# One of sixteen P slabs and one of sixteen dS slabs per attention head: transposed on TensorE instead of by the DMA crossbar

## The chip, the cores and the metric

The kernel runs on one core of one Trainium2 chip. The metric is device time in microseconds, one number per execution. All runs quoted here are of the same state, called fast, and are medians of several executions. The kernel before was run again beside every set of experiments. Its median moved between 5479 and 5498 us from set to set, so kernels of different sets are compared by their ratio to the kernel before of the same rounds, not by their microseconds. A ratio is the mean time of one kernel's fast runs over the mean of the other's fast runs of the same rounds, so it is not quite the ratio of the two medians quoted.

## The reference

The reference is the forward and backward pass of attention gated by a gated linear unit; only attention matters here. It has 32 heads, 2048 queries, 2048 cached keys, head size 128:

```python
q = (x @ wq).reshape(B, Sq, H, Dh).transpose(0, 2, 1, 3)
scores = jnp.einsum("bhqd,bhkd->bhqk", q, k_cache) * Dh ** -0.5
p = softmax(scores)
o = jnp.einsum("bhqk,bhkd->bhqd", p, v_cache)
# ... and the gradients of x, k_cache, v_cache, wq, wo and the gated unit's weights
```

The backward pass needs, per head, `dP = dO V^T`, `dS = P * (dP - delta)`, `dQ = dS K`, `dK = dS^T Q`, `dV = P^T dO`.

## The kernel before

A head is 32 *slots*: 16 P slots, then 16 dS slots, one for each slab of 128 queries. A P slot computes one slab `Pq` (128 x 2048 bf16) of exponentials. A dS slot overwrites it with dS. The products O and dQ need the slab transposed, and one DMA through the crossbar does that for each of the 32 slabs:

```python
def transpose_slab(hs, qt, name):
    T = wpt.tile([P, NT, P], bf, name=name, tag="PT")      # 7 buffers
    nc.sync.dma_start_transpose(T[:], hs.slabs[qt][:])
    return T
```

The transposed slab is used five slots later (`skew = 5`) by a *tail* of 16 matmuls. Each slot also has its share of dV and dK, which read the slab untransposed. From dS slot 6 of a head on, the next one is prepared (the code is cut at each `...`):

```python
def plan(h):
    b1, b2 = 2 * NT * h, 2 * NT * h + NT         # first P slot, first dS slot
    ...
    put(pl + q(skew + 1), 0, lambda: heads.__setitem__(h, prep_loads(h)))   # loads K, V, wq, wo
    put(pl + q(skew + 3), NT * P, lambda: prep_kt(hd()))
    ...
    for qt in range(NT):
        put(b1 + qt + skew, ..., lambda qt=qt: tail1(hd(), qt, 0))          # O
    ...
        put(b2 + qt + skew, ..., lambda qt=qt: tail2(hd(), qt, 0))          # dQ

def prep_loads(h):
    ...
    hs.Vn = ld1.tile([P, NT, P], bf, name="Vn")                             # one buffer
    nc.gpsimd.dma_start(hs.Vn[:], A_v_cache[0, h].rearrange("(p t) d -> p t d", t=NT))   # 512 KB
```

`Vn` has one buffer, so its load for the next head waits for the last O tail, which runs in dS slot 4.

## Time and profile before

| What | Where it is read | Value |
|---|---|---|
| time | three runs | 5479 us (5477 to 5485) |
| attention stage | first and last slot in the timeline | 608 to 3883 us |
| one head | starts of the slots, heads 1 to 30 | mean 103.0 us, median 102.0 us |
| TensorE busy in the stage | windows | 95% |
| pitch (start to start) of 128-column matmuls | starts in the timeline | 55.8 ns |
| TensorE idle per head, by releaser | idle before instructions, heads 2 to 28 | dST 1.9, PT 0.8, VectorE's dS multiply 1.6, small gaps 1.1 us |

The windows of the kernel before, heads 4 to 27. After the length come the busy microseconds of TensorE, its weight loads, VectorE, ScalarE and GpSimd, then the granted clock (the share of TensorE's full clock that the profile records), the DMA share (the packets' time as a share of 16 engines' time, over 1 where packets overlap) and GB/s:

```profile
1012.00:3487.00 2475.00, 2348.21 (x29909) 1868.24 (x30389) 1409.92 (x3154) 1612.02 (x2727) 771.92 (x1325) 1.00 1.14 199
```

TensorE is 2348 / 2475 = 95% busy. The costliest groups of the kernel before; after the bars stand busy time, mean duration, and TensorE's idle time before them with its releaser:

```profile
L535 PE MATMUL dp<-VT,dOT 128*128 128x512 bf16 x1728 | 541.5, 380 | 53.7 <-DVE Pq L538 53.6
L510 PE MATMUL acc<-Kn,dST 128*128 128x128 bf16 x8192 | 554.0, 220 | 69.3 <-DMA dST<-Pq 65.6
L510 PE MATMUL acc<-Vn,PT 128*128 128x128 bf16 x8192 | 547.8, 219 | 33.0 <-DMA PT<-Pq 25.6
```

The dQ tails waited 66 us and the O tails 26 us for a landing from the crossbar, over all heads. The timeline of SP, the engine that issues the transposes, shows why (start, length, count):

```profile
1147.04 25.15 SPq L460 DMA_TRANSPOSE PT<-Pq  x9
1172.29 53.55 SPq L460 DMA_TRANSPOSE dST<-Pq  x16
1225.92 49.98 SPq L460 DMA_TRANSPOSE PT<-Pq  x16
1276.00 15.35 SPq L460 DMA_TRANSPOSE dST<-Pq  x4
```

There is no gap: 16 transposes take 50 to 54 us, the length of the 16 slots. From the end of the instruction that finishes a slab to the issue of its transpose, a P slab waits 3.8 us and a dS slab 4.8 us in the median. So two resources are nearly full, TensorE and the transposing queue.

### The profile page before, as it was taken

The page shows a single profiled execution, that of the slowest core. Times are in us where ns is not written, and L with a number is a line of the kernel's source. Part 1 is how long each engine was busy: PE and PEld are TensorE (multiplying, and loading weights), DVE is VectorE, ACT ScalarE, POOL GpSimd, SP SyncE. Part 2 cuts the span into 40 slices and gives each one's busy share as a digit, 9 for nine tenths or more (in the row PEclk, how much of TensorE's full clock was granted, in tenths as well). Part 3 has the DMA queues.
Part 4 walks back from the last instruction along what each step waited for, and adds up shares of the span by engine and source line. Part 5 has one row for each costly group of instructions (what it writes and reads, how often), then busy time and mean ns, then how long its engine had stood idle before and what let it go on. Part 6 is the DMA issues. An engine that isn't in the chain of part 4 may idle for free. (4 is left out here: it accounts for less than half of the span.)

```text
span 5498.0 us, 129982 instructions
## 1 busy us (share of the span) xinstructions
PE 5095.5 (93%) x54343; PEld 3654.3 (66%) x55220; DVE 2497.0 (45%) x5692; ACT 2695.0 (49%) x4794; POOL 1420.1 (26%) x2361
## 2 busy tenths in 40 slices
PE   8878899999999999999999999999789999899999
PEld 3334577777777777777777777777557777644454
DVE  4443455655655555655556555555333333210011
ACT  7751466666666666666666666666222222100000
POOL 2212323323333233333233233223112222211000
PEclk9999999999999999999999999999999999999999
DMA  7658799999999999999999999999945455674865
GB/s 282 235 187 194 155 199 189 204 196 201 200 200 198 200 198 193 200 205 199 201 200 199 188 199 198 200 198 189 236 143 195 167 174 180 199 219 120 172 146 111
DMA packets 2721787, 1053.95 MB, mean 192 GB/s; under 512 B 2521937, under 2 KB 2642386, under 8 KB 2719138
## 3 DMA queue, kind: packets, MB, share of 16 engines
q1 hardware_dynamic: 2637890, 764.83, 76.0%
q0 software_dynamic: 83296, 280.64, 16.6%
q8 instruction: 434, 7.11, 0.5%
q14 instruction: 167, 1.37, 0.1%
HBM read 213.91 MB, written 201.00 MB: 75 GB/s over the span
## 5 line engine op out<-in xcount | busy, mean ns | idle before, releaser
L484 ACT ACTIVATE Pq<-sp 128x1024 bf16<-128x1024 f32 x1024 | 1048.1, 1024 | 328.2 <-PE sp L466 205.5
L570 PEld LDWEIGHTS <-Pq 128*128 128x128 bf16 x16384 | 1002.5, 98 | 241.2 <-issue 2.1
L542 ACT ACTIVATE t<-dp,negdelta 128x1024 bf16<-128x1024 f32 x512 | 571.5, 1116 | 278.9 <-POOL negdelta L524 160.7
L538 DVE SCALAR_TENSOR_TENSOR Pq<-dp,delta,Pq 128x1024 bf16<-128x1024 f32 x512 | 655.0, 1279 | 58.1 <-PE acc L510 56.4
L510 PE MATMUL acc<-Kn,dST 128*128 128x128 bf16 x8192 | 554.0, 220 | 69.3 <-DMA dST<-Pq 65.6
L510 PEld LDWEIGHTS <-PT 128*128 128x128 bf16 x8192 | 498.8, 98 | 156.4 <-DMA PT<-Pq 47.8
L543 DVE TENSOR_TENSOR Pq<-t,Pq 128x1024 bf16<-128x1024 bf16 x512 | 419.1, 819 | 398.1 <-ACT t L542 394.9
L535 PE MATMUL dp<-VT,dOT 128*128 128x512 bf16 x1728 | 541.5, 380 | 53.7 <-DVE Pq L538 53.6
L510 PEld LDWEIGHTS <-dST 128*128 128x128 bf16 x8192 | 490.4, 98 | 140.3 <-DMA dST<-Pq 85.7
L510 PE MATMUL acc<-Vn,PT 128*128 128x128 bf16 x8192 | 547.8, 219 | 33.0 <-DMA PT<-Pq 25.6
L570 PE MATMUL acc<-dOn,Pq 128*128 128x128 bf16 x8192 | 546.5, 219 | 10.3 <-DVE o_n L50 0.2
L466 PE MATMUL sp<-KT,QT 128*128 128x512 bf16 x1762 | 547.7, 379 | 1.2 <-ACT Pq L484 1.2
L570 PE MATMUL acc<-Qn,Pq 128*128 128x128 bf16 x8192 | 541.3, 219 | 3.4
L499 POOL TENSOR_SCALAR dOn<-dOn,rinv_all 128x128 bf16<-128x128 bf16 x512 | 313.9, 613 | 612.0 <-DVE rinv_all L472 502.9
L552 ACT ACTIVATE dq_n<-acc,rsc 128x128 bf16<-128x128 f32 x512 | 188.3, 368 | 401.8 <-PE acc L510 401.8
L800 PEld LDWEIGHTS <-xn_all 128*128 128x128 bf16 (+1 forms) x2880 | 281.5, 100 | 40.3 <-issue 11.1
L50 DVE TENSOR_SCALAR o_n<-acc,rinv_all 128x128 bf16<-128x128 f32 x352 | 123.5, 351 | 299.3 <-PE acc L510 299.3
L580 POOL DMA_DIRECT2D out_dram<-kvo x256 | 148.9, 582 | 406.3 <-DVE kvo L579 404.0
L276 PE MATMUL g_ps<-wg_sb,xnT 128*128 128x512 bf16 x694 | 185.8, 392 | 59.8 <-ACT oma L282 50.2
L504 POOL DMA_DIRECT2D dq_d<-dq_n x128 | 98.3, 768 | 497.5 <-ACT dq_n L552 479.7
L535 PEld LDWEIGHTS <-dOT 128*128 128x128 bf16 x2048 | 164.3, 98 | 83.0 <-issue 61.0
L881 ACT ACTIVATE dxn<-acc 128x512 f32<-128x512 f32 (+1 forms) x32 | 12.7, 411 | 420.8 <-PE acc L872 420.8
(182 smaller groups left out, 7163.6 us busy)
## 6 DMA issues: line engine op xcount, KB each, us to landing
out_dram<-kvo POOLq DMA_DIRECT2D x256, 128.0 KB, 4.6
h_d<-h_row POOLq DMA_DIRECT2D x48, 384.0 KB, 4.3
a_d<-a_row POOLq DMA_DIRECT2D x48, 384.0 KB, 3.1
b_d<-b_row POOLq DMA_DIRECT2D x48, 384.0 KB, 5.2
a_blk<-a_d SPq DMA_DIRECT2D x18, 1024.0 KB, 5.8
b_blk<-b_d SPq DMA_DIRECT2D x18, 1024.0 KB, 18.9
h_blk<-h_d POOLq DMA_DIRECT2D x18, 1024.0 KB, 11.4
du_d<-du_blk POOLq DMA_DIRECT2D x18, 1024.0 KB, 9.1
```

What stands on the lines that cost most here:

```text
L276: nc.tensor.matmul(g_ps[:], lhsT=xnT[:kk, i, srows], rhs=wg_sb[:kk, i, fs], start=(i == 0), stop=(i == DT - 1))
L466: nc.tensor.matmul(sp[:, c * CH:(c + 1) * CH], lhsT=hs.QT[:, qt * P:(qt + 1) * P], rhs=hs.KT[:, hf * HW_ + c * CH: hf * HW_ + (c + 1) * CH ...
L484: nc.scalar.activation(Pq[:, hsl], sp[:], AF.Exp, scale=SCALE, accum_out=hs.rsp[:, hf:hf + 1])
L499: nc.gpsimd.tensor_scalar(hs.dOn[:, qt, :], hs.dOn[:, qt, :], hs.rinv_all[:, qt:qt + 1], None, op0=ALU.mult)
L510: nc.tensor.matmul(hs.acc[:, 0, :], lhsT=T[:, kt, :], rhs=rhs[:, kt, :], start=(kt == 0), stop=(kt == NT - 1))
L535: nc.tensor.matmul(dp[:, c * CH:(c + 1) * CH], lhsT=hs.dOT[:, qt * P:(qt + 1) * P], rhs=hs.VT[:, hf * HW_ + c * CH: hf * HW_ + (c + 1) * C ...
L538: nc.vector.scalar_tensor_tensor(Pq[:, hsl], dp[:], hs.delta[:, qt:qt + 1], Pq[:, hsl], op0=ALU.subtract, op1=ALU.mult)
L542: nc.scalar.activation(t[:], dp[:], AF.Identity, bias=hs.negdelta[:, qt:qt + 1], scale=1.0)
L543: nc.vector.tensor_tensor(Pq[:, hsl], t[:], Pq[:, hsl], op=ALU.mult)
L552: nc.scalar.activation(hs.dq_n[:, qt % G4, :], hs.acc[:, 0, :], AF.Copy, scale=hs.rsc[:, qt:qt + 1])
L570: nc.tensor.matmul(self.tile[:, j, :], lhsT=self.slabs[qt][:, kt * P:(kt + 1) * P], rhs=self.rhs[:, qt, :], start=(qt == self.lo), stop=(q ...
L800: nc.tensor.matmul(acc[:kd, :], lhsT=xn_all[:, st, d0:d0 + kd], rhs=blk_[:, st, :], start=(st == 0), stop=(st == NT - 1))
```

## The change

The intent is to relieve the queue: slab 7 of P and of dS are transposed on TensorE, 16 matmuls against the identity each, and evicted from PSUM by VectorE (P) or ScalarE (dS).

```diff
+            on_pe = {NTH - 1} if fast else set()
+
             def transpose_slab(hs, qt, name):
+                if qt in on_pe:
+                    return None
                 T = wpt.tile([P, NT, P], bf, name=name, tag="PT")
                 nc.sync.dma_start_transpose(T[:], hs.slabs[qt][:])
                 return T
+
+            def pe_slab(hs, qt, dst, name, g, eng):
+                if g == 0:
+                    dst[qt] = wpt.tile([P, NT, P], bf, name=name, tag="PT")
+                T = dst[qt]
+                pe_transpose_blocks(lambda j: hs.slabs[qt][:, j * P:(j + 1) * P], g, min(g + 8, NT),
+                                    lambda k, n: T[:, k:k + n, :], eng)
@@ main1
-                    hs.nm = stat.tile([P, NHF], f32, name="nm")
+                    hs.nm = None if fast else stat.tile([P, NHF], f32, name="nm")
@@ plan
+                for qt in on_pe:
+                    for g in range(0, NT, 8):
+                        put(b1 + qt + 2 + g // 8, ..., lambda ...: pe_slab(hd(), qt, hd().PT, "PT", g, "v"))
+                        put(b2 + qt + 2 + g // 8, ..., lambda ...: pe_slab(hd(), qt, hd().dST, "dST", g, "s"))
```

More of the change, by code (lines that the diff above doesn't have):

```diff
@@ L623, in plan @@
                         put(pl + q(skew + 4 + 2 * sc), DT * CH, lambda sc=sc: prep_qt(hd(), sc))
+                for qt in on_pe:
+                    for g in range(0, NT, 8):
+                        put(b1 + qt + 2 + g // 8, NT * P // 2, lambda qt=qt, g=g: pe_slab(hd(), qt, hd().PT, "PT", g, "v"))
+                        put(b2 + qt + 2 + g // 8, NT * P // 2, lambda qt=qt, g=g: pe_slab(hd(), qt, hd().dST, "dST", g, "s"))
                 for qt in range(NT):
```

## The prediction

> **What bounds the kernel now.** The 32-head attention stage runs from 608 to 3883 us of the 5498 us span; a head lasts 102.9 us (mean of heads 2 to 29). Two resources are almost full in it. (1) TensorE: the windows show it 95% busy. By pitch of matmul starts, a 128-column matmul costs 55.8 ns and a 512-column one 216 ns; one head's 1088 and 168 of them, and 5 for Wo, make an estimated 97.5 us. (2) The transposing DMA queue: in SP's timeline the 32 transposes of a head follow each other with 0.09 us between (only near P slabs 1 to 3 does the queue run dry, under 1 us per head), one each 3.1 us; a finished slab waits 4 to 8 us before its transpose is issued.
>
> TensorE's idle time is 5.5 us per head (idle before instructions, by releaser): 2.7 us wait for a crossbar landing (1.9 for dST, 0.8 for PT, mostly in P slots 8 to 15 and dS slots 0 to 9), 1.6 us for VectorE's dS multiply at dS slots 1 and 2, and 1.1 us of small gaps. The 1.6 us are not the crossbar's: there the 3.6 us Qn multiply on GpSimd runs, a VectorE multiply beside it takes 2.84 instead of 0.69 us, and dp has no free PSUM buffer.
>
> **What the change does, per head.** It takes 2 of 32 transposes from the queue: 2 x 3.1 = 6.2 us of queue time; 30 x 3.1 = 94 us of a 102 us head leaves slack. It adds 32 TensorE transposes. The Trainium skill (TensorE: Matmul & The Clock Gate, Part 4) gives 275 to 390 ns for one; this trace shows 219 ns duration but a 55.8 ns pitch in the existing groups of 16 (KT, VT, Qn). So +32 x 55.8 ns = +1.8 us of TensorE. It adds two 128x1024 evictions on VectorE in the P phase (0.68 us each) and two on ScalarE in the dS phase (1.02 us each); both have room (57% and 65% busy). The dropped nm tile is unused on the fast path.
>
> **On the critical path.** All +1.8 us lies there, TensorE being nearly full. What can be won is only the 2.7 us of crossbar waits. P slab 7 leaves the queue just as the backlog starts to bite, and relieves everything up to dS slots 6 to 8, where most waits are, by about 3 us; dS slab 7's relief comes after the waits and goes mostly unused. I expect 0.3 to 0.5 us of crossbar wait to remain. Net: 2.7 - 0.4 - 1.8 = 0.5 us per head, about 16 us in 32 heads, 0.3%.
>
> **Predicted:** 5462 us, 8 in 10 within 5432 to 5490. Faster by over 2%: 0.03; within 2%: 0.95; slower by over 2%: 0.02.
>
> **What would show it.** Head period near 102.4 us; TensorE's idle for DMA PT and dST under 0.7 us per head; the wait for the dS multiply still about 1.6 us; the transpose queue idle 4 to 6 us per head; 960 transposes issued; the added transposes at a 56 ns pitch; the other stages unchanged within 5 us.
>
> **What would make it wrong.** Faster: if less crossbar traffic also speeds the other waits; even all of the 2.7 us gone saves only 30 us. Slower: the new groups take PSUM accumulators (4 in rotation) in slots that already hold Qn (P slot 10) and next-head K and Q preparation (dS slots 8 to 11); if VectorE or ScalarE evicts late, TensorE waits for an accumulator, and a new wait of 1 us per head turns the gain into a loss. A clock granted lower in a few heads (108 to 111 us in three of them now) moves single runs by some 10 us.

## More of the kernel before

One more view of the kernel before was not looked at closely enough when the prediction was made, the instructions on the V tile:

```profile
L399 POOL DMA_DIRECT2D Vn<-in_A_v_cache_dram x32: 547/602/612, 594.6 to 3748.2; - x32
DMA to landing us min/median/max: 4.4/5.6/15.4
```

A V load lands in 5.6 us as a rule, but the slowest took 15.4.

## The result, and the profile after

The changed kernel takes 5562 us (5558 to 5564, four runs) against 5482 us for the kernel before in the same rounds: ratio 1.0142, 95% interval 1.0124 to 1.0159. It is 1.4% slower, outside the stated range. A later control run of it on another occasion gave 1.0112 (1.0085 to 1.0138).

The lines that answer to those of before:

```profile
L546 PE MATMUL dp<-VT,dOT 128*128 128x512 bf16 x1757 | 554.6, 384 | 96.0 <-DVE Pq L549 95.9
L521 PE MATMUL acc<-Kn,dST 128*128 128x128 bf16 x8192 | 555.1, 220 | 46.8 <-DMA dST<-Pq 43.3
L521 PE MATMUL acc<-Vn,PT 128*128 128x128 bf16 x8192 | 546.8, 219 | 7.0 <-DMA PT<-Pq 0.2
L590 DVE TENSOR_TENSOR kvo<-acc,part 128x512 bf16<-128x512 f32 x256 | 176.3, 689 | 146.6 <-DMA out_dram<-kvo 86.0
```

The wait for PT is gone, 25.6 to 0.2 us, as intended. The wait for dST is not: 43 us. The wait of dp for VectorE's dS multiply has grown from 54 to 96 us, and VectorE now waits 86 us for the stores of dV and dK to leave their buffers (26 us before, in the view of that tile). All in all TensorE idles as long as before, 5.4 against 5.5 us per head, and has 57 us more to do. SP's timeline in the same stretch as above:

```profile
1148.66 14.25 SPq L464 DMA_TRANSPOSE PT<-Pq  x5
1163.50 50.73 SPq L464 DMA_TRANSPOSE dST<-Pq  x15
1215.60 50.73 SPq L464 DMA_TRANSPOSE PT<-Pq  x15
```

Now there are breaks, 0.6 and 1.4 us between these rows. A row hides the breaks inside it: summed from the starts and ends of all slab transposes, gaps of over 0.15 us make 628 us, against 37 us before. The queue runs dry, as intended.

The mean hides that there are two kinds of heads. Twelve of heads 1 to 30 last 101.5 to 101.7 us, shorter than the median head of before (102.0). The other 18 last 103 to 113 us. In 17 of these 18 the V load of dS slot 4 took over 8 us, and in none of the twelve. Here is the timeline of one bad head around dS slot 4, then of one good head (start, length, instruction, from narrow windows):

```profile
1703.84 3.81 SPq L464 DMA_TRANSPOSE dST<-Pq  x1
1704.33 0.60 POOL L399 DMA_DIRECT2D Vn<-in_A_v_cache_dram  x1 [1.40 <-PE acc L521]
1707.74 8.76 SPq L464 DMA_TRANSPOSE dST<-Pq  x1
1716.60 3.72 SPq L464 DMA_TRANSPOSE dST<-Pq  x1
...
2016.77 4.04 SPq L464 DMA_TRANSPOSE dST<-Pq  x1
2020.55 0.60 POOL L399 DMA_DIRECT2D Vn<-in_A_v_cache_dram  x1 [1.40 <-PE acc L521]
2020.90 4.12 SPq L464 DMA_TRANSPOSE dST<-Pq  x1
2025.11 3.63 SPq L464 DMA_TRANSPOSE dST<-Pq  x1
```

In the bad head a transpose was issued 0.5 us ahead of the V load, and the next transpose, issued in the midst of it, takes 8.8 us instead of 4. In the good head the transposes fall otherwise and nothing is slow. The windows of ten microseconds of each, with the same columns as above:

```profile
1706.00:1716.00 10.00, 8.53 (x119) 7.04 (x118) 6.18 (x8) 5.43 (x7) 1.75 (x3) 1.00 1.16 123
2022.00:2032.00 10.00, 9.89 (x141) 8.36 (x140) 8.69 (x11) 5.77 (x8) 2.46 (x4) 1.00 1.13 247
```

The DMA engines are as busy in the bad stretch (1.16) as in the good one (1.13) and move half as much, 123 against 247 GB/s. V load, transposes and the stores of dV and O that happen to be in flight are all slow together. I call this a *collision* and count a V load that takes over 8 us. The kernel before has 2 in 31 heads, the changed kernel 17. Its V loads:

```profile
L399 POOL DMA_DIRECT2D Vn<-in_A_v_cache_dram x32: 545/600/609, 588.0 to 3813.6; - x32
DMA to landing us min/median/max: 4.3/8.6/15.4
```

What follows in the bad head is visible in the same timeline, in TensorE's rows that began with idle time:

```profile
1716.46 1.07 PE L521 MATMUL acc<-Kn,dST 128*128 128x128 bf16 x16 [1.83 <-DMA dST<-Pq]
1718.98 1.01 PE L546 MATMUL dp<-VT,dOT 128*128 128x512 bf16 x2 [1.45 <-DVE Pq L549]
1722.34 0.62 PE L378 MATMUL acct<-ident,Pq 128*128 128x128 bf16 x8 [0.22 <-issue]
```

The dQ tail of dS slot 8 waits for the transpose that was issued 0.5 us ahead of the V load: it landed at 1716.42 us, 12.6 us after its issue, where 5.5 us is the median of its tile. The dS multiply is late too, because VectorE stood 4.1 us in front of a dV result whose buffer was still being stored (that store landed at 1716.92 us, and the instruction began at 1717.04; the profile's own view names TensorE for this wait). Then the granted clock falls:

```profile
1712.00:1716.00 4.00, 2.58 (x35) 1.98 (x33) 0.69 (x1) 1.72 (x3) 0.00 (x0) 1.00 1.26 136
1716.00:1720.00 4.00, 2.09 (x21) 1.42 (x22) 2.48 (x3) 0.37 (x1) 1.29 (x2) 0.87 1.25 165
1720.00:1724.00 4.00, 3.78 (x47) 3.45 (x47) 1.43 (x2) 3.12 (x4) 0.00 (x0) 0.71 1.23 289
```

(The third number from the end is the granted clock.) In 15 of the 18 bad heads the clock is halved for 3.4 to 10.2 us in or next to dS slot 8. Weighted by what it withholds, that is 49.5 us of the attention stage, 35 us of it while TensorE was busy; in the kernel before it is 11.9 us, 8 us of it while TensorE was busy. The Trainium skill (TensorE: Matmul & The Clock Gate, "Why this matters for your kernels") advises to leave no idle gap over about 3 us between bursts of matmuls, since a window of idleness halves the clock. A halved clock with idle time just before it is what this trace shows too; the length of the gap does not agree, for in this head two gaps of 1.83 and 1.45 us came before it.

### The profile page after: what moved, and what is told of

Same layout as the page of the kernel before. It is cut to its first block, busy times and chain, and to the rows that moved or that the text cites. A ratio compares the mean times of both kernels' runs of the same rounds, so it can differ in the third digit from the quotient of the medians.

```text
span 5561.9 us, 132038 instructions
## 1 busy us (share of the span) xinstructions
PE 5170.7 (93%) x55335; PEld 3740.3 (67%) x56244; DVE 2543.2 (46%) x5756; ACT 2747.3 (49%) x4858; POOL 1415.3 (25%) x2361
## 4 chain that ended last, share of the span: by engine, by line
PE 78%; DMA 8%; issue 5%; ACT 4%; DVE 2%; SPq 2%; POOL 1%; ACTq 0%; DVEq 0%; POOLq 0%
PE acc L581 15%; PE acc L521 14%; PE acc L887 7%; PE sp L477 6%; PE dp L546 6%; PE accw L815 6%; PE acc L436 5%; PE acct L378 4%; DMA out_dram<-kvo 3%; PE dh L792 3%; PE acc L324 3%; PE accq L855 2%; PE accd L804 2%; PE acc L846 2%; PE acc L754 2%
## 5 line engine op out<-in xcount | busy, mean ns | idle before, releaser
L549 DVE SCALAR_TENSOR_TENSOR Pq<-dp,delta,Pq 128x1024 bf16<-128x1024 f32 x512 | 655.2, 1280 | 55.9 <-PE dp L546 27.8
L546 PE MATMUL dp<-VT,dOT 128*128 128x512 bf16 x1757 | 554.6, 384 | 96.0 <-DVE Pq L549 95.9
L521 PE MATMUL acc<-Kn,dST 128*128 128x128 bf16 x8192 | 555.1, 220 | 46.8 <-DMA dST<-Pq 43.3
L581 PE MATMUL acc<-dOn,Pq 128*128 128x128 bf16 x8192 | 546.1, 219 | 10.2
L590 DVE TENSOR_TENSOR kvo<-acc,part 128x512 bf16<-128x512 f32 x256 | 176.3, 689 | 146.6 <-DMA out_dram<-kvo 86.0
```

The costliest lines, as they stand in the source:

```text
L521: nc.tensor.matmul(hs.acc[:, 0, :], lhsT=T[:, kt, :], rhs=rhs[:, kt, :], start=(kt == 0), stop=(kt == NT - 1))
L546: nc.tensor.matmul(dp[:, c * CH:(c + 1) * CH], lhsT=hs.dOT[:, qt * P:(qt + 1) * P], rhs=hs.VT[:, hf * HW_ + c * CH: hf * HW_ + (c + 1) * C ...
L549: nc.vector.scalar_tensor_tensor(Pq[:, hsl], dp[:], hs.delta[:, qt:qt + 1], Pq[:, hsl], op0=ALU.subtract, op1=ALU.mult)
L581: nc.tensor.matmul(self.tile[:, j, :], lhsT=self.slabs[qt][:, kt * P:(kt + 1) * P], rhs=self.rhs[:, qt, :], start=(qt == self.lo), stop=(q ...
```

## The experiments

**Theory 1 (collision).** With two transposes less the queue runs dry. A dS transpose is then issued the moment its slab is ready, and not when the queue gets to it. Slab and V load are both released by the compute engines, so their distance in time becomes fixed, 0.5 us in 18 of 31 heads, and that happens to be a bad distance. In the kernel before the backlog spread it over 0 to 3.5 us. The traces bear out the first half of this: from slab ready to transpose issued, dS slabs 0 to 3 wait 2.8 to 5.3 us in the kernel before and 0.0 to 0.1 us in the changed one (each slab's median over the heads).

**Theory 2 (cost).** The added TensorE groups, their PSUM accumulators, and the ScalarE evictions, which fall into dS slots 9 and 10 right after the preparation of the next K, push the schedule; the slow transfers come along with that.

In the table, V loads over 8 us are counted in the one profiled run of each kernel. "Quiet head" is the shortest of heads 1 to 30.

| Run | Ratio to before (95%) | Median us | Slow V loads of 31 | Quiet head us |
|---|---|---|---|---|
| the changed kernel | 1.0142 (1.0124 to 1.0159) | 5562 | 17 | 101.5 |
| the same, control | 1.0112 (1.0085 to 1.0138) | 5551 | 14 | 101.5 |
| P slab only | 1.0075 (1.0041 to 1.0108) | 5531 | 16 | 100.6 |
| dS slab only | 0.9977 (0.9942 to 1.0012) | 5479 | 2 | 100.9 |
| relief alone | 0.9999 (0.9968 to 1.0030) | 5483 | 14 | 99.7 |
| cost alone | 1.0033 (1.0008 to 1.0058) | 5511 | 2 | 101.5 |
| V load 0.4 us later | 0.9980 (0.9941 to 1.0018) | 5487 | 6 | 101.5 |
| V load behind the O store | 0.9967 (0.9931 to 1.0003) | 5475 | 3 | 101.5 |
| V load in dS slot 11 | 0.9937 (0.9910 to 0.9964) | 5455 | 0 | 101.5 |
| before, V load in dS slot 11 | 1.0001 (0.9973 to 1.0028) | 5487 | 2 | 99.7 |
| P slab only, V load behind the O store | 0.9940 (0.9920 to 0.9959) | 5464 | 8 | 100.6 |
| P slab only, V load in dS slot 11 | 0.9907 (0.9880 to 0.9933) | 5445 | 6 | 100.6 |
| both paths into one tile | 1.0725 (1.0693 to 1.0758) | 5889 | 15 | 111.9 |

**1. The V load moved away.** The load now waits for the dQ tail of dS slab 6, by way of a one-element copy into the V tile (cut here: the two lines leave `prep_loads`, and head 0 calls `load_vn` without `after`):

```diff
+            def load_vn(hs, after=None):
+                hs.Vn = ld1.tile([P, NT, P], bf, name="Vn")
+                if after is not None:
+                    nc.gpsimd.tensor_copy(hs.Vn[0:1, 0, 0:1], after)
+                nc.gpsimd.dma_start(hs.Vn[:], A_v_cache[0, hs.h].rearrange("(p t) d -> p t d", t=NT))
@@ tail2
+                if qt == 6 and hs.h + 1 < H:
+                    load_vn(heads[hs.h + 1], hs.dq_n[0:1, qt % G4, 0:1])
```

> The changed kernel, with the next head's V load (512 KB from HBM) held back from dS slot 4 to after the dQ tail of dS slab 6 (dS slot 11). Theory 1 (collision): in the changed kernel the transposing queue runs dry, dS transposes are issued at a fixed moment against the V load, and load and transposes slow each other in 17 of 31 heads (V lands in 8 to 15 us instead of 4.5, one transpose issue takes 7 to 14 us, TensorE stalls 2 to 9 us in dS slot 8 and its clock is halved after it). Then with the load elsewhere no transpose issue of dS slots 3 to 5 takes over 6 us, all heads last about 101.5 us and the time is 5440 to 5460 us. Theory 2 (cost): the added TensorE groups, their accumulators and the ScalarE evictions in dS slots 8 to 10 make the loss, and the slow transfers only come along: the time stays at 5550 to 5565 us.

Measured: 5455 us, ratio 0.9937: faster than the kernel before, where the change without this edit is slower. No V load takes over 6.3 us, and the mean head is 101.65 us. The lines that answer to the two views above:

```profile
L525 PE MATMUL acc<-Kn,dST 128*128 128x128 bf16 x8192 | 551.2, 219 | 5.1 <-DMA dST<-Pq 1.5
L550 PE MATMUL dp<-VT,dOT 128*128 128x512 bf16 x1757 | 545.9, 379 | 62.2 <-DVE Pq L553 62.2
...
DMA to landing us min/median/max: 4.2/4.4/6.3
```

The dST wait is gone (43.3 to 1.5 us) and the dS multiply's is back near its old size. The two profiles also give the price of the collisions. The attention stage is 3347.8 - 3233.6 = 114 us shorter. TensorE's idle time in dS slots 6 to 9, summed over heads 0 to 30, falls from 81.7 to 3.2 us, and what the clock withheld while TensorE was busy from 35 us to nothing (no half clock is left between the first and the last slot): 78 + 35 = 113 us.

**2. The same edit on the kernel before.**

> The kernel before, with the same late V load. Theory 1: the four heads of it that show the collision (periods 103 to 111 us) lose it, and the waits for dST in dS slots 6 to 8 (1.8 us a head) shrink: 5430 to 5465 us. Theory 2: nothing to gain, 5475 to 5485 us.

Measured: 5487 us, ratio 1.0001. This is a miss for theory 1 as I had put it. The wait for dST did halve, from 1.9 to 0.9 us per head in the profile, but the wait for PT rose from 0.8 to 1.1, and two loads in the new place took over 8 us. Theory 2's "nothing to gain" came true here, though its reason is refuted below. With the queue full, taking one disturbance away leaves the queue full. The collisions are few in this kernel, and the V load is not what limits it.

**3. Relief alone.** Slab 7's two transposes are left out with nothing in their place, so the result is wrong:

```diff
                 if qt in on_pe:
-                    return None
+                    return (hs.PT if name == "PT" else hs.dST)[qt - 1]
@@ plan: the calls of pe_slab are removed
```

> Wrong result on purpose: the two crossbar transposes of slab 7 are left out and nothing is put in their place (the tails of slab 7 read the transposed slab 6). Relief alone, without the TensorE cost of 57 us. Theory 1: the queue runs dry as in the changed kernel, so the collision shows in 8 or more of 31 heads, and the time is only about 57 us under the changed kernel: 5490 to 5520 us, slower than before in spite of less work. Theory 2: with no added work there is no loss; the crossbar waits go and the time falls to 5395 to 5430 us.

Measured: 5483 us, ratio 0.9999, a little below the range given for theory 1 and far from theory 2. A kernel with strictly less work than the kernel before is not faster. It has 14 slow V loads. Its quiet heads last 99.7 us, 1.8 us less than the changed kernel's, which is 32 transposes at 55.8 ns: TensorE's cost is as it was costed.

**4. Cost alone, first attempt.** TensorE transposes slab 7 once more, into the tile that the crossbar has filled.

```diff
-                if qt in on_pe:
-                    return None
@@ pe_slab
-                if g == 0:
-                    dst[qt] = wpt.tile([P, NT, P], bf, name=name, tag="PT")
```

> The kernel before plus cost alone: slab 7 is transposed by the crossbar as before and then once more on TensorE into the same tile, with the evictions. Theory 1: the queue stays as full as before, few heads collide, and the added 57 us of TensorE are partly hidden in the crossbar waits: 5500 to 5540 us. Theory 2: cost without relief must be at least as slow as the changed kernel: 5560 to 5600 us.

Measured: 5889 us, ratio 1.0725, outside both expectations; the experiment was badly made. The eviction must wait until the crossbar's write of the same tile has landed, TensorE then waits for the eviction (4.5 us per head for ScalarE's, 2.9 us for VectorE's), and at 115 us per head the queue ran dry here as well, with 15 slow loads. It says nothing on cost.

**5. Cost alone, done better.** As before, but the TensorE groups are evicted into a scratch tile that nobody reads.

```diff
-                if g == 0:
-                    dst[qt] = wpt.tile([P, NT, P], bf, name=name, tag="PT")
-                T = dst[qt]
+                T = wscr.tile([P, NT, P], bf, name="scr")
```

> Cost alone, done better than the run in which both paths wrote one tile: all 32 slabs go by the crossbar, and TensorE transposes P and dS slab 7 once more into a scratch tile that nobody reads. Theory 1: the queue stays full, V loads over 8 us in under 7 heads; TensorE's 57 us are partly hidden in the crossbar waits of 2.7 us a head: 0.2 to 1.0% slower than before. Theory 2 (the added groups and evictions are what costs): as slow as the changed kernel or slower, 1.4% or more.

Measured: 5511 us, ratio 1.0033. The queue stays full, two V loads are slow, and the full cost of the change, evictions and accumulators included, makes the kernel 0.3% slower, about 18 us of the 57. The rest is hidden in waits. Theory 2 needed 1.4% or more.

**6. One slab at a time.** The set `on_pe` is split in two, `{NTH - 1}` for one kind of slab and empty for the other.

> Only dS slab 7 is transposed on TensorE; P slab 7 goes by the crossbar as before. Theory 1: the relief comes after dS slot 4, so the queue is as full there as before and few heads collide (under 7 of 31); half of the added cost (29 us) is paid, some of it hidden in waits: 5485 to 5515 us. Theory 2, in the form that is left (the dS-side TensorE groups and ScalarE evictions beside the K preparation make the loss): most of the 80 us appears here, 5535 to 5560 us.

> Only P slab 7 is transposed on TensorE, dS slab 7 goes by the crossbar, V load where it was. Theory 1: it is the relief in the P phase that empties the queue ahead of dS slot 4, so the collision stays (V load over 8 us in 10 or more heads) and the time is the changed kernel's less half of the added cost, 29 us: 0.5 to 1.2% slower than before. If the collision needs both reliefs, it vanishes: 0.3 to 0.9% faster than before.

Measured: with the dS slab alone 0.9977 and 2 slow V loads; with the P slab alone 1.0075 and 16 slow loads. The dS slab carries the evictions that theory 2 blamed, and by itself it does no harm (it came out a little faster than I had expected). The P slab alone brings the collisions. This is the order of events that theory 1 needs: P slab 7 leaves the queue ahead of the next dS slot 4, dS slab 7 after it. It is also the sharpest test of *when* against *how many*: both kernels leave the queue idle equally long in their profiles (263 us with the dS slab alone, 262 us with the P slab alone). But dS slabs 0 to 3 wait 1.6 to 2.8 us for their transpose with the dS slab alone, and 0.0 to 0.3 us with the P slab alone.

**7. The load shifted by less than a microsecond.** A GpSimd memset of the V tile precedes its load: 256 columns (the load comes 0.4 us later), or 512 columns, which in the built program also puts the O store ahead of the load.

```diff
                 hs.Vn = ld1.tile([P, NT, P], bf, name="Vn")
+                nc.gpsimd.memset(hs.Vn[:, 0:2, :], 0.0)        # 0:4 in the second kernel
                 nc.gpsimd.dma_start(hs.Vn[:], ...)
```

> The changed kernel with a small GpSimd memset of the V tile ahead of its load: the load is issued about 0.3 us later, in the same dS slot 4. Theory 1a (phase): it is the timing against the transposes that matters: heads collided where a transpose was issued 0.5 us (changed kernel) or 1.1 to 1.3 us (kernel before) ahead of the V load. With a transpose 0.8 us ahead the collision stays in 10 or more of 31 heads: 5535 to 5580 us. Theory 1b (overlap only: any V load that meets the O and dV stores and dS transposes of these slots is at risk, whatever the exact moment): the same here.

> The same with a memset of 512 columns, which puts the O store of dS slot 4 ahead of the V load: the load is issued some 1.5 to 2.5 us later than in the changed kernel, still in dS slots 4 to 5 and beside the same stores. Theory 1a (phase): the last transpose is then 2 to 3 us ahead of the load and the next under 1 us behind it, as in the undisturbed heads: under 4 collided heads of 31, 5445 to 5475 us. Theory 1b (overlap only): the load still meets stores and transposes: 10 or more collided heads, 5530 to 5570 us.

Measured: 0.9980 with 6 slow loads, and 0.9967 with 3. The second went as the phase theory said; its time is 0.3% under that of before, though the interval reaches 1.0003. In the first I was wrong about the width of the bad phase. I had taken it from the slowest V loads of before, where the transpose was 1.1 to 1.3 us ahead, and expected 10 or more slow loads with 0.8 us; shifting the load by 0.4 us was enough to bring them from 14 to 17 down to 6. That rules out the plain form "any load that meets these stores and transposes is at risk", and it leaves the phase as the thing that matters, though not with the sharp edges that I had drawn.

Over the three profiles in which the load was left in its place and P slab 7 was taken off the queue (the changed kernel, its control, P slab only), 93 loads: where the last transpose was issued 0.4 to 0.6 us ahead of the load, 47 of 54 loads took over 8 us; in all other cases, none of 39. This window was drawn after these loads had been seen. Two traces that were not used for it agree with it: 12 of 15 inside and 2 of 16 outside for relief alone, 15 of 15 and 0 of 16 for both paths into one tile. But the six slow loads of the run shifted by 0.4 us lie at 0.28 to 0.86 us, so the distance is not the whole condition.

**8. The control, and two versions that beat both kernels.**

> The changed kernel unaltered, as a control beside the other runs of this call, because the runs of the kernel before differ between chips by some tenths of a per cent. Both theories: 1.0 to 1.8% slower than before; by theory 1 the V load of dS slot 4 takes over 8 us in 10 or more of 31 heads.

> Only P slab 7 on TensorE, and the V load behind the 512-column memset and the O store, as in the run that nearly ended the collisions. Theory 1: V loads over 8 us in under 5 heads, quiet heads of 100.6 us, 0.5 to 1.0% faster than before, near the run with P slab alone and the late V load (0.93% faster).

> Only P slab 7 is transposed on TensorE, and the V load is late. The late V load alone with both slabs had heads of 101.5 us; leaving the dS slab to the crossbar takes away 16 transposes at 55.8 ns, 0.9 us a head. If the dS relief came after the waits and went unused, as the prediction said, quiet heads last 100.6 us and the time is 5420 to 5435 us, the fastest so far. If the dS relief is needed for the P phase of the next head, waits for PT come back and the time is 5450 us or more.

Measured: the control is 1.1% slower than before, with 14 slow loads, so the loss is no accident of one occasion. P slab alone with the load behind the O store: 0.9940, in the expected range, but with 8 slow loads (one of them at 8.004 us) where I had said under 5. P slab alone with the load in dS slot 11: 5445 us, ratio 0.9907 (5498 us for the kernel before in those rounds), the lowest ratio of all, though its interval overlaps those of the two at 0.994. Its median was 10 us over the range I gave, while the kernel before was also slow in those rounds. The dS relief was indeed not needed: quiet heads last 100.6 us, 0.9 us less than with both slabs, and the PT wait stays at 0.3 us per head. Six of its V loads are still slow, now in dS slot 11, and some heads of 104 to 108 us remain, so it is not at its floor.

**What stays open.** Why the DMA engines move half as much in a collision was not found. The trace shows that they are as busy as in an undisturbed stretch and that everything in flight is slow, not which of the transfers holds up which. Nor is it known why the transposes of the changed kernel fall 0.5 us ahead of the V load in 18 heads and otherwise, mostly 3.8 us ahead, in the rest.

## Why the prediction was wrong

- *Added TensorE time, 1.8 us per head, all on the critical path*: right in size. The trace shows a pitch of 55.9 ns for the new groups, and quiet heads of 99.7, 100.6 and 101.5 us with none, 16 and 32 of these transposes. The Trainium skill (TensorE: Matmul & The Clock Gate, Part 1) gives 55.8 ns for 128 columns at the full clock, and this trace agrees. Not all of it is critical in a kernel that still waits: the cost alone took about 18 of 57 us.
- *Crossbar waits of 2.7 us per head are what can be won*: right for an undisturbed kernel. With the V load out of the way they fall to almost nothing, and the kernel is 0.63% faster, about 35 us, near the 30 us that the prediction gave for "all of the 2.7 us gone".
- *"I expect 0.3 to 0.5 us of crossbar wait to remain"*: this is the step that failed, and with it the assumption that all other waits stay as they are ("the wait for the dS multiply still about 1.6 us"). The PT wait went to zero, but 1.2 us of dST wait remained per head, the wait for the dS multiply went from 1.6 to 3.0 us, and the clock withheld 27 us more of TensorE's busy time. In place of 0.5 us won, the mean head became 2.5 us longer (103.0 to 105.5 us in the profiles). The cause was a transfer that the prediction did not consider: removing transposes changes not only how many there are but *when* the others are issued, and with the queue dry they fell at a fixed, bad distance from the V load.
- *"A clock granted lower in a few heads (108 to 111 us in three of them now) moves single runs by some 10 us"*: the evidence lay here and was taken for noise. In two of these heads, 14 and 23, the V load took 10.7 and 15.4 us; the low clock came with the stalls in dS slots 7 and 8. (The third, head 3, lost its clock in a P slot.) The same event, in two heads of 31, became the rule in the changed kernel.
- *The queue idle 4 to 6 us per head*: it was idle about 20 us (628 us over 32 heads). The heads were longer, and a transpose took 2.8 us in the mean, less than the 3.1 us that I had read from a full queue.
- *Waits for accumulators as the risk*: did not appear; TensorE waited for no PSUM accumulator of the new groups.
- *960 transposes, other stages unchanged within 5 us*: right, but for the stretch before the first slot, which is 7 us shorter in the profile of the changed kernel; after the last slot it is 2 us shorter.

Summed up from the two profiles: +57 us of TensorE work, +27 us withheld by the clock while TensorE was busy, and an unchanged idle time (176 us in the stage in both) make +84 us; the attention stage grew by 73 us. The 11 us between them are not accounted for. The profiled execution of the kernel before (span 5498 us) was also about 20 us longer than the median of its other runs.

## What to carry to other kernels

A queue with a backlog hides when its entries become ready; take the backlog away and the transfers lock to the compute engines, so look at what else is issued at that moment before counting the relief as gain. If a few periods of a repeated schedule are long, find what was slow in them before calling them noise, because a change of phase can make that the common case. A large plain load can be moved away, by a dependency, from the stretch where transposes are about to be waited for; here that paid once the queue had run dry (0.9937) and not while it was full (1.0001). Test such a suspicion by shifting the load a fraction of a microsecond: it costs one line.

## What the Trainium skill lacked or had wrong

- DMA: Bandwidth & Descriptors, "Rules for kernel authors", says that a transpose next to ordinary DMAs needs nothing. For the result this holds: all runs with both were correct but the one that was wrong on purpose. For the time it lacks what the runs show: a 512 KB load beside transposes and stores took 8 to 16 us instead of 4.5, the core moved 123 instead of 247 GB/s, and one transpose took 8.8 us to issue instead of 4. The page names no such slowdown and no dependence on the phase.
- TensorE: Matmul & The Clock Gate, "Why this matters for your kernels", warns of idle gaps over about 3 us. Here two gaps of 1.83 and 1.45 us, about 1 us apart, were followed by 3.4 us at half clock; in another head, 1.17 and 1.62 us before the half clock at 1398 us.
- The same page, Part 4, gives 275 to 390 ns for one TensorE transpose. In groups of 8 and 16 here one lasts 219 ns and they follow each other every 55.9 ns; the page lacks that a series of them costs no more than other 128-column matmuls.
